# Scan and mixture of adapters on one core: transposes in pairs, stores in 8 KB rows, a copy in words

## The chip, the cores and the metric

The kernel runs on one core of a Trainium2 chip. The core has five engines that work side by side, each through its own list of instructions and in that list's order: TensorE (PE in the profile), VectorE (DVE), ScalarE (ACT), GpSimd (POOL) and SyncE (SP), which issues most of the transfers. Sixteen DMA engines carry them. The metric is the time of one execution on the device in microseconds; smaller is better. A time is given as the median of several runs.

## The reference

A linear recurrence over 8 sequences of 6400 tokens with 128 channels gives x, and a mixture of eight rank-16 adapters, two of them chosen for each token, is added to it:

```python
for t in range(S):
    h = a[:, t] * h + b[:, t]
    out[:, t] = h
...
logits = x @ w_gate
topk = np.argpartition(-logits, K, axis=1)[:, :K]
...
        z = x[mask] @ A[e]
        delta[mask] += w[mask, k, None] * (z @ B[e])
return (x + delta).astype(np.float32)
```

K is 2 and w is the softmax over the two largest logits. `a`, `b` and the output are float32 of 26.2 MB each, 51200 tokens by 128 channels.

## The kernel before

**Chunks.** The 51200 tokens are 100 chunks of 512. For a chunk c the work is a chain of small steps, and the program names each step by a family and a number:

- `la`, `lb`: the loads of a and b, a pair of chunks in each (512 KB, 128 partitions with a 4 KB row each, line 396). Six buffers of a and six of b; a load waits until PE has read the buffer's earlier pair. The first four chunks come singly.
- `A`, `B`: PE turns a chunk to channels by tokens with transposes against the identity, into two banks `pA` and two banks `pB` (line 417). From chunk 4 on, B of chunk c and A of chunk c+1 are woven into one step `P`c of 16 transposes: P4 is B4 with A5, P5 is B5 with A6. `P`c waits for the copy of A(c-1) and the scan of c-2, which free the banks.
- `ae`: ACT copies pA to SBUF (line 435). `sc`: DVE scans, out of that copy and of pB, into `xT` as 16-bit numbers (line 482), chunk after chunk.
- `Z`, `ze`: one matmul for each block of 128 tokens gives the eight adapters' inner vectors and the logits (line 500), six blocks in a unit; ACT copies them to the ring `zl` (line 506).
- `g1` to `g8`, `gx`, `w1`: the gates of a group of four units (24 blocks), in seven small steps on DVE or POOL and a sigmoid on ACT (lines 534 to 554).
- `mu`: the inner vectors times the gates, in 16 bits, POOL or DVE (line 569).
- `T`, `te`: PE transposes that in 16 bits (line 578), and ACT or DVE copies it from PSUM to `zwT` (lines 582 and 583, with the helper at line 300). `D`: x and the adapters' output are summed in PSUM with eight matmuls (lines 588 and 589). `T` and `D` share one of two banks `pO`.
- `oe`: ACT or DVE copies the bank to the ring `outt` (line 602, helper 300). `st`: SP stores it (line 631).

**Order.** Nothing is scheduled when it runs. `ORDER` (lines 28 to 100) lists for each engine the steps in the order in which it takes them, and where a step may run on either of two engines the list in which it stands decides (`te` and `oe` on ACT or DVE; `mu` and the gates on POOL or DVE). `Program.waits` derives the semaphore waits from the dependences. So an engine whose next step isn't ready holds up everything behind it in its list, and SP's list holds loads and stores together.

**Rings and stores.** `STORES` says how many chunks a store takes: 48 stores of two chunks and four of one. The tokens of a stored tile are dealt out in runs, one run to a partition, so that each partition stores one row: `Z` of a block therefore waits for the scans of the whole tile in which it lies. `NX`, `NZ` and `NO` are the sizes of the rings `xT` (24 chunks), `zl` (120 blocks) and `outt` (72 blocks). `SPLIT` cuts one store by partitions, 124 and 4. `FILL` puts four more PE transposes of the identity, read by nobody, ahead of the transposes of a for each of chunks 7 to 14 (`fi7` to `fi14`, line 446).

Of the kernel before, what the change touches and what calls it, by code (L numbers as in the profile page):

```python
# [12 lines left out]
STORES = [2] * 48 + [1] * 4  # L13
SPLIT = {68: [124, 4]}
TOP8 = 4
WARM = 16
FILL = {k: 4 for k in range(7, 15)}
# [3 lines left out]
NX = 24  # L21
NZ = 120
NO = 72
# [3 lines left out]
TAIL_CHUNKS = 12  # L27
ORDER = {
# [16 lines left out]
    ),  # L45
    "act": (
# [60 lines left out]
class Program:  # L107
# [18 lines left out]
    def schedule(self):  # L126
        named = {op.name: op for op in self.ops}
        assert len(named) == len(self.ops)
        self.order = {e: [named[name] for name in ORDER[e].split()] for e in self.ENGINES}
        assert sum(len(o) for o in self.order.values()) == len(self.ops)  # L130
        for e in self.ENGINES:
            n = 0
            for op in self.order[e]:
# [597 lines left out]
```

## Time and profile before

| | |
|---|---|
| time, median of 3 runs | 201.59 us (201.13 to 202.28) |
| the profiled execution, its time | 201.01 us |
| its span, from first to last instruction | 199.2 us |
| granted TensorE clock over the span | 0.994 |
| bytes moved by DMA | 79.26 MB |
| read from HBM, written to HBM | 52.56 MB, 26.21 MB |
| instructions | 7709 |

The profile is of one execution. Its first part gives each engine's busy time. The second cuts the span into 40 slices of 4.98 us. Another part lists the DMA queues with the number of their packets, the megabytes and the time these took as a share of sixteen engines' span. Groups of instructions are listed with what one of them takes. Views by stretch give the same busy times for any part of the span, where the column ahead of the last is the DMA engines' busy share; a share may come out a little over 1 because packets follow each other with a small overlap. A busy PE is modelled: matmuls are pipelined, and each is shown with its whole latency, so that the distance from one start to the next says more than the busy share.

### The profile page before, as it was taken

What the parts mean: (1) busy time and instruction counts of PE and PEld (TensorE: products, weight loads), DVE (VectorE), ACT (ScalarE), POOL (GpSimd) and SP (SyncE); (2) the same over time, 40 slices, a digit from 0 to 9 for tenths busy, and PEclk for the clock granted to TensorE, in tenths of its full rate; (3) what the DMA queues carried; (4) which work ended last, traced back from release to release, by engine and by line L of the source; (5) the groups of instructions that cost most, each with busy time, mean ns of one, the idle gap of its engine ahead of it and who ended that gap; (6) DMA issues with size and microseconds to landing.
All of it is one profiled execution on the core that took longest, in us unless ns stands there. A gap on an engine that the chain in (4) does not pass through costs nothing.

```text
span 199.2 us, 7709 instructions
## 1 busy us (share of the span) xinstructions
PE 185.2 (93%) x3224; PEld 165.5 (83%) x3224; DVE 175.0 (88%) x291; ACT 176.9 (89%) x327; POOL 136.0 (68%) x168
## 2 busy tenths in 40 slices
PE   6899999999998979999999999999999999999990
PEld 6778888889987968899989989889988978878970
DVE  1599999989999879799999999999999899899980
ACT  2378699999988979899999999999999989999981
POOL 3210186878786657969989998796598978676520
PEclk9999999999999999999999999999999999999997
DMA  5999999999999999999999999999999999999796
GB/s 214 385 414 406 410 407 407 409 406 410 411 410 413 414 411 412 415 414 408 414 415 406 411 410 416 411 411 415 414 412 414 417 410 412 406 393 392 298 405 254
DMA packets 22921, 79.26 MB, mean 398 GB/s; under 512 B 2664, under 2 KB 2920, under 8 KB 22888
## 3 DMA queue, kind: packets, MB, share of 16 engines
q1 hardware_dynamic: 22312, 78.39, 98.1%
q8 instruction: 25, 0.41, 0.8%
q10 hardware_dynamic: 576, 0.40, 0.6%
q14 instruction: 8, 0.07, 0.1%
HBM read 52.56 MB, written 26.21 MB: 395 GB/s over the span
## 4 chain that ended last, share of the span: by engine, by line
PE 80%; ACT 5%; DMA 4%; issue 3%; SPq 2%; POOL 2%; DVE 1%; DVEq 0%
PE pB L417 23%; PE pO L588 13%; PE pZ L500 13%; PE pO L578 12%; PE pO L589 10%; PE pA L417 5%; DMA a_tm<-in_a_dram 4%; ACT outt L300 3%; PE pA L446 2%; SPq L396 2%; POOL zw L569 2%; ACT zwT L300 1%; ACT a_st L435 1%; ACT zl L506 1%; DVE xT L482 1%
## 5 line engine op out<-in xcount | busy, mean ns | idle before, releaser
L482 DVE TENSOR_TENSOR_SCAN xT<-a_st,xT,pB 128x512 f16<-128x512 f32 x96 | 120.4, 1254 | 6.6 <-PE pA L417 3.1
L569 POOL TENSOR_TENSOR zw<-zl,g 128x512 f16<-128x512 f32 x90 | 94.5, 1065 | 29.2 <-DVE g L554 23.2
L417 PE MATMUL pB<-ident_f,b_tm 64*128 64x64 f32 (+1 forms) x784 | 67.5, 229 | 1.2 <-issue 0.5
L417 PE MATMUL pA<-ident_f,a_tm 64*128 64x64 f32 (+1 forms) x784 | 67.8, 229 | 0.6 <-issue 0.4
L435 ACT COPY a_st<-pA 128x512 f32<-128x512 f32 x100 | 59.0, 613 | 7.9 <-PE pA L417 7.2
L417 PEld LDWEIGHTS pB<-ident_f,b_tm 64*128 64x128 f32 (+1 forms) x784 | 55.8, 139 | 10.9 <-issue 3.4
L506 ACT COPY zl<-pZ 128x816 f32<-128x816 f32 (+1 forms) x69 | 58.1, 842 | 1.7 <-PE pZ L500 1.6
L588 PE MATMUL pO<-ident_h,xT 128*128 128x128 f16 x368 | 55.2, 233 | 2.0 <-issue 1.8
L417 PEld LDWEIGHTS pA<-ident_f,a_tm 64*128 64x128 f32 (+1 forms) x784 | 56.0, 139 | 1.2 <-DMA a_tm<-in_a_dram 0.7
L300 ACT COPY outt<-pO 128x512 f32<-128x512 f32 x87 | 52.2, 609 | 4.6 <-PE pO L589 4.1
L589 PE MATMUL pO<-cst_h,zwT 128*128 128x128 f16 x368 | 53.0, 219 | 1.7 <-issue 1.7
L588 PEld LDWEIGHTS pO<-ident_h,xT 128*128 128x128 f16 x368 | 46.3, 144 | 4.9 <-issue 2.1
L589 PEld LDWEIGHTS pO<-cst_h,zwT 128*128 128x128 f16 x368 | 39.6, 108 | 1.8 <-issue 1.8
L500 PE MATMUL pZ<-cst_h,xT 128*128 128x136 f16 x400 | 37.8, 229 | 0.5 <-issue 0.4
L578 PE MATMUL pO<-ident_h,zw 128*128 128x128 f16 x368 | 35.5, 220 | 1.1 <-POOL zw L569 0.4
L500 PEld LDWEIGHTS pZ<-cst_h,xT 128*128 128x128 f16 x400 | 30.6, 145 | 1.5 <-DVE cst_h L324 0.2
L578 PEld LDWEIGHTS pO<-ident_h,zw 128*128 128x128 f16 x368 | 22.3, 97 | 5.5 <-POOL zw L569 1.3
L300 DVE COPY zwT<-pO 128x512 f16<-128x512 f16 x56 | 23.0, 414 | 3.5 <-PE pO L578 3.1
L300 ACT COPY zwT<-pO 128x512 f16<-128x512 f16 x36 | 21.4, 600 | 0.9 <-PE pO L578 0.8
L545 POOL TENSOR_TENSOR L<-L,k 128x192 f32<-128x192 f32 x14 | 8.8, 631 | 4.6 <-DVE L L543 4.0
L482 DVE TENSOR_TENSOR_SCAN xT<-a_st,pB 128x512 f16<-128x512 f32 (+1 forms) x8 | 7.5, 938 | 4.5 <-PE pB L417 4.4
L548 POOL TENSOR_TENSOR k<-k,L 128x192 f32<-128x192 f32 (+1 forms) x17 | 9.1, 535 | 2.5 <-DVE L L539 1.8
(56 smaller groups left out, 120.0 us busy)
## 6 DMA issues: line engine op xcount, KB each, us to landing
a_tm<-in_a_dram SPq DMA_DIRECT2D x48, 512.0 KB, 13.3
b_tm<-in_b_dram SPq DMA_DIRECT2D x48, 512.0 KB, 13.4
out_dram<-outt SPq DMA_DIRECT2D x47, 512.0 KB, 11.9
a_tm<-in_a_dram SPq DMA_DIRECT2D x4, 256.0 KB, 4.9
out_dram<-outt SPq DMA_DIRECT2D x4, 256.0 KB, 4.0
b_tm<-in_b_dram SPq DMA_DIRECT2D x3, 256.0 KB, 5.6
out_dram<-outt SPq DMA_DIRECT2D x1, 496.0 KB
b_tm<-in_b_dram ACTq DMA_DIRECT2D x1, 256.0 KB, 4.0
```

Of the source, the lines that this page charges most:

```text
L300: return e.copy(dst, src) if e is eng["act"] else e.tensor_copy(dst, src)
L417: last = e.transpose(*args)
L435: lambda e: e.copy(a_st[c % NA][:, :], pA[:, c % 2, :]))
L482: last = e.tensor_tensor_scan(out=x[:, s0:s1], data0=a_st[c % NA][:, s0:s1], data1=pB[:, c % 2, s0:s1], initial=init, op0=ALU.mult, op1=AL ...
L500: last = e.matmul(pZ[:, k // (n // 2), o : o + W], xblock(b0 + k), Awg_h)
L506: lambda e: e.copy(zl[:, zb : zb + n, :].rearrange("p (h k) w -> p h (k w)", h=2), pZ[:, :, 0 : n // 2 * W]))
L545: d3 = wide(5, [d3], lambda e: e.tensor_tensor(out=ll, in0=ll, in1=kk, op=ALU.add))
L548: d6 = wide(7, [d2, d5], lambda e: e.tensor_tensor(out=kk, in0=kk, in1=ll, op=ALU.add))
L569: lambda e: e.tensor_tensor(out=wv, in0=zv, in1=gv, op=ALU.mult))
L578: last = e.transpose(ptile[:, k * 128 : k * 128 + 128], zz[:, k, :], ident_h[:, :])
L588: e.matmul(dst, xblock(b0 + k), ident_h[:, :], start=True, stop=False)
L589: last = e.matmul(dst, zt[:, k * 128 : k * 128 + 128], B_h, start=False, stop=True)
```

## The change

The diff has five parts.

1. `STORES` becomes [2,2], sixteen of four chunks, [2,2], six of four and four of one: 30 stores in place of 52. A store of four chunks has rows of 8 KB on each partition. The tiles of `xT` and `outt` follow. The rings become `NX` 32 chunks, `NO` 96 blocks, `NZ` 80 blocks.
2. `te` on ACT copies the 512 16-bit numbers of a partition as 256 words of 32 bits. On DVE it stays as it was.
3. `FILL` is two in place of four.
4. The lists of all five engines are new. On PE, P5 and P6, P7 and P8, and so on to P97 and P98 stand next to each other, so that A of both chunks of a transfer is turned in one stretch. By counting the lists: ACT has 69 `te` (38 before) and 82 `oe` (95); DVE has 31 `te` (62), 18 `oe` (5) and 15 `mu` (10); POOL has 85 `mu` (90); of the gates' steps g2, g3, g5, g6 and g7 DVE has 6, 11, 5, 7 and 8 (9, 6, 3, 7 and 5). PE goes from 32-bit to 16-bit operands or back 107 times (155).
5. `AHEAD`, `TREE` and `MASK` bring code that isn't reached with the values given (1000, empty, empty): no list of SP is 1000 steps long.

```diff
-STORES = [2] * 48 + [1] * 4
+STORES = [2,2]+[4]*16+[2,2]+[4]*6+[1]*4
-FILL = {k: 4 for k in range(7, 15)}
+FILL = {k:2 for k in range(7,15)}
-NX = 24
-NZ = 120
-NO = 72
+NX = 32
+NZ = 80
+NO = 96
 ORDER = {
     "pe": (
-        "P41 P42 D23 T24 Z26 P43 T25 D24 Z27 D25 T26 P44 P45 Z28 D26 T27 P46 Z29 T28 D27 D28 Z30 P47 T29 T30 P48 D29 "
+        "T23 Z25 T24 D23 D24 Z26 T25 T26 D25 P43 P44 T27 D26 D27 T28 Z27 P45 P46 T29 Z28 D28 D29 P47 P48 T30 T31 Z29 "
...
-        "Z60 D74 D75 P93 Z61 T77 T76 P94 P95 D76 D77 Z62 T78 P96 T79 Z63 D78 D79 T80 T81 Z64 D80 D81 P97 T82 Z65 T83 "
-        "D82 D83 T84 P98 T85 D84 Z66 D85 T86 B99 T87 Z67 T90 D86 D87 T91 Z68 T88 T89 D91 D88 D90 T92 D89 T93 T94 D92 "
+        "T75 P93 P94 T76 D75 Z60 D76 T77 P95 P96 T78 Z61 D77 D78 Z62 T79 T80 Z63 D79 D80 Z64 T81 P97 P98 T82 D81 D82 "
+        "T83 T84 D83 Z65 D84 T85 B99 D85 T86 Z66 T87 D86 D87 Z67 T88 T90 T91 T89 D88 Z68 D90 T93 D89 D91 T92 T94 D93 "
...
     "sp": (
-        "la20 la24 la22 st0 lb22 la26 lb24 lb26 la28 la30 lb30 st2 lb28 lb34 la32 la34 lb32 lb36 la36 st6 st4 lb38 "
+        "lb20 lb22 la22 la24 lb26 lb24 la26 la28 lb28 st2 st0 lb30 la30 la32 st4 lb32 la34 lb34 lb36 la36 la38 lb38 "
...
-        "la84 st46 lb84 st48 la86 la88 lb86 lb88 st50 la90 st52 lb90 st54 la92 lb92 la94 st56 lb94 la96 st58 lb96 "
-        "st60 la98 st62 st72 st64 lb98 st66 st68 st78 st76 st70 st74 st82 st80 st86 st84 st90 st88 st92 st94 st96 "
-        "st97 st98 st99 "
+        "la76 lb76 st32 la78 lb78 la80 lb80 la82 lb82 la84 lb84 st40 la86 lb86 la88 lb88 st44 la90 lb90 la92 lb92 "
+        "st48 la94 lb94 st52 la96 lb96 st56 la98 lb98 st60 st68 st70 st64 st72 st80 st76 st84 st88 st92 st97 st96 "
+        "st99 st98 "
...
-            o_te[c] = P.add("dve act", f"te{c}", J, [o_T[c]] + get(o_D, c - NW),
-                            lambda e: copy(e, zt, ptile[:, 0:C]))
+            o_te[c] = P.add("dve act", f"te{c}", J // 2, [o_T[c]] + get(o_D, c - NW),
+                            lambda e: e.copy(zt.bitcast(F32), bank[:, 0 : C // 2]) if e is eng["act"]
+                            else e.tensor_copy(zt, ptile[:, 0:C]))
```

More of the change, by code (lines that the diff above doesn't have):

```diff
@@ L12 @@
 GROUPS = [1, 2] + [4] * 15 + [2, 1, 1, 1, 1]
-STORES = [2] * 48 + [1] * 4
-SPLIT = {68: [124, 4]}
+STORES = [2,2]+[4]*16+[2,2]+[4]*6+[1]*4
+SPLIT = {68:[124,4]}
 TOP8 = 4
 WARM = 16
-FILL = {k: 4 for k in range(7, 15)}
+FILL = {k:2 for k in range(7,15)}
 HEAD = 4
@@ L27 @@
 TAIL_CHUNKS = 12
+AHEAD = 1000
+TREE = ()
+MASK = ()
 ORDER = {
     "pe": (
[15 rows of a table removed]
[15 rows of a table added]
     ),
     "act": (
[16 rows of a table removed]
[17 rows of a table added]
     ),
     "dve": (
[14 rows of a table removed]
[13 rows of a table added]
     ),
     "pool": (
[8 rows of a table removed]
[8 rows of a table added]
     ),
     "sp": (
[8 rows of a table removed]
[7 rows of a table added]
     ),
@@ L130, in schedule @@
         assert sum(len(o) for o in self.order.values()) == len(self.ops)
+        for before, op in zip(self.order["sp"], self.order["sp"][AHEAD:]):
+            op.deps = op.deps + [before]
         for e in self.ENGINES:
@@ L552, in gating @@
                     zlast[zpos[u] + k] = d5 if top else d2
-            o_g[gi] = wide(8, [a1, d5] + (get(o_mu, glast[gi - NG]) if gi >= NG else []),
-                           lambda e: e.scalar_tensor_tensor(
-                               out=gg, in0=ll, scalar=0.0, in1=sg, op0=ALU.is_ge, op1=ALU.mult))
+            free = get(o_mu, glast[gi - NG]) if gi >= NG else []
+            if gi in MASK:
+                d8 = wide(9, [d5, d6], lambda e: e.tensor_scalar(
+                    out=ll, in0=ll, scalar1=0.0, scalar2=1.0, op0=ALU.is_ge, op1=ALU.mult))
+                o_g[gi] = P.add("pool dve", f"gf_{gi}", nb, [a1, d8] + free,
+                                lambda e: e.tensor_tensor(out=gg, in0=ll, in1=sg, op=ALU.mult))
+            else:
+                o_g[gi] = wide(8, [a1, d5] + free, lambda e: e.scalar_tensor_tensor(
+                    out=gg, in0=ll, scalar=0.0, in1=sg, op0=ALU.is_ge, op1=ALU.mult))
         def back(gi, c):
```

108 rows, old and new, of the table ORDER are left out of this document.

## Prediction, before the result was known

> **What bounds the kernel now.** I read the page first: the DMA row of its slices and the queues, then the chain.
>
> ```profile
> span 199.2 us, 7709 instructions
> ...
> PE 185.2 (93%) x3224; PEld 165.5 (83%) x3224; DVE 175.0 (88%) x291; ACT 176.9 (89%) x327; POOL 136.0 (68%) x168
> ...
> DMA  5999999999999999999999999999999999999796
> GB/s 214 385 414 406 410 407 407 409 406 410 411 410 413 414 411 412 415 414 408 414 415 406 411 410 416 411 411 415 414 412 414 417 410 412 406 393 392 298 405 254
> ...
> q1 hardware_dynamic: 22312, 78.39, 98.1%
> ...
> PE 80%; ACT 5%; DMA 4%; issue 3%; SPq 2%; POOL 2%; DVE 1%; DVEq 0%
> ...
> a_tm<-in_a_dram SPq DMA_DIRECT2D x48, 512.0 KB, 13.3
> ```
>
> The queue that carries every load and store is busy for 98.1% of the span, and from the third slice to the thirty-fifth the rate never leaves 406 to 417 GB/s. That flatness is what to see: a transfer rate that doesn't move while the work on the engines changes is a ceiling. The chain names PE for 80%, but it follows one path only, and a load takes 13.3 us from issue to landing, ten times the 1.27 us that 512 KB need at 412 GB/s: about ten transfers stand in the queue. What PE releases late is late in a queue that isn't empty.
>
> Then the engines, stage by stage (PE, PEld, DVE, ACT, POOL with instructions, the clock, the DMA share, the rate).
>
> ```profile
> 90.00:110.00 20.00, 19.91 (x380) 18.24 (x379) 19.57 (x26) 19.98 (x38) 18.59 (x24) 1.00 1.02 411
> 110.00:130.00 20.00, 19.72 (x376) 17.91 (x375) 19.14 (x30) 19.66 (x38) 17.41 (x22) 1.00 1.03 412
> ...
> 170.00:180.00 10.00, 9.44 (x150) 7.88 (x148) 9.11 (x24) 9.50 (x18) 7.74 (x8) 1.00 0.99 398
> 180.00:190.00 10.00, 9.87 (x152) 9.14 (x153) 9.82 (x36) 10.00 (x23) 5.61 (x8) 1.00 0.86 345
> 190.00:199.20 9.20, 4.00 (x60) 3.24 (x57) 3.28 (x14) 4.14 (x10) 0.47 (x1) 0.88 0.83 324
> ```
>
> ACT and DVE are nearly full too, so compute is a close second, and in the last 20 us the order turns round: ACT is full (10.00 of 10) while the DMA share falls to 0.86. So DMA bounds the kernel up to about 172 us, and compute bounds the tail. The forecast is the DMA's work plus what the DMA idles at the end.
>
> **Stores in 8 KB rows: minus 1.8 us of DMA work.** No store of before has 8 KB rows, so I take the price of a row from two stretches, one with 4 KB rows only (60 to 80 us) and one with 2 KB rows (the last stores, 195 to 197 us).
>
> ```profile
> q1 hardware_dynamic: 2248, 8.19, 101.4%
> ```
>
> ```profile
> q1 hardware_dynamic: 416, 0.77, 101.3%
> ```
>
> 8.19 MB are 2000 rows of 4 KB; 1.014 x 16 engines x 20 us = 324.5 us of packet time, or 162.2 ns a row. 0.77 MB are 376 rows of 2 KB; 1.013 x 16 x 2 us = 32.4 us, 86.2 ns a row. Two rows of 2 KB cost 172.4, so joining two rows saves 10.2 ns. The change has 22 stores of four chunks, 22 x 128 = 2816 joins: 2816 x 10.2 ns / 16 engines = **1.8 us**. The bounds: nothing, if an 8 KB row moves as two pieces, and 2.0 us by the rounding of 0.77 MB (0.765 MB is 373.5 rows, 86.8 ns each, 11.4 ns a join). I take 1.8.
>
> The Trainium skill, DMA: Bandwidth & Descriptors, section "Why small descriptors are slow", puts the overhead at about 3 cycles a packet. At the 850 MHz that its section "Where 436 GB/s comes from" gives, an estimate by that page is 3.5 ns a join and 0.6 us in all; the rows show three times that, and the measurement decides.
>
> **The tail: minus 1.2 us.** The DMA view from 160 us to the end has slices of 0.98 us.
>
> ```profile
> GB/s 397 401 414 422 422 414 414 405 410 414 426 422 414 376 359 393 368 405 414 414 393 389 389 426 339 288 247 359 192 405 405 418 405 401 410 385 380 395 94 4
> ```
>
> Against 412 GB/s the nine low slices (376 359 393 368 at 173 to 177 us, 339 288 247 359 192 at 183 to 188) lack 787 GB/s of a slice: 787 / 412 x 0.98 = 1.9 us in which the DMA had nothing to send. SP's queue in that stretch:
>
> ```profile
> 158.68 6.11 SPq L631 DMA_DIRECT2D out_dram<-outt  x3
> 164.83 0.45 SPq L396 DMA_DIRECT2D b_tm<-in_b_dram  x1
> 165.32 30.18 SPq L631 DMA_DIRECT2D out_dram<-outt  x19
> ```
>
> The last load (lb98) goes out at 164.83, behind three stores that took 6.11 us. In the new list lb98 stands ahead of st60: 60 chunks are stored before it in place of 66, so the last input comes 6 x 0.64 = 3.8 us sooner (0.64 us is a chunk's 262 KB at 412 GB/s), and 40 chunks of stores remain to cover the rest of the compute instead of 34. Against it: PE's list has 19 `D` left behind P98 (D81 to D99) where it had 16. ACT's busy time after 180 us is 10.00 + 4.14 = 14.1 us for 16 chunks, 0.9 us each; three more are 2.7 us. Net 1.1 us sooner. I take 1.2 of the 1.9, bounds 0 and 1.9; st80 now stands ahead of st76, so a late oe83 would hold two stores.
>
> **What the edits do to the engines; worth nothing by itself while DMA is the bound.**
>
> ```profile
> L506 ACT COPY zl<-pZ 128x816 f32<-128x816 f32 x62 | 53.7, 867 | 1.1 <-PE pZ L500 1.0
> L300 ACT COPY outt<-pO 128x512 f32<-128x512 f32 x87 | 52.2, 609 | 4.6 <-PE pO L589 4.1
> L300 DVE COPY zwT<-pO 128x512 f16<-128x512 f16 x56 | 23.0, 414 | 3.5 <-PE pO L578 3.1
> L300 ACT COPY zwT<-pO 128x512 f16<-128x512 f16 x36 | 21.4, 600 | 0.9 <-PE pO L578 0.8
> L569 DVE TENSOR_TENSOR zw<-zl,g 128x512 f16<-128x512 f32 x10 | 6.8, 684 | 0.0
> L506 ACT COPY zl<-pZ 128x544 f32<-128x544 f32 x7 | 4.4, 624 | 0.6 <-PE pZ L500 0.6
> L446 PE MATMUL pA<-ident_f 128*128 128x128 f32 x32 | 5.0, 279 | 0.0
> L300 DVE COPY outt<-pO 128x512 f32<-128x512 f32 x5 | 3.4, 674 | 0.5 <-PE pO L589 0.5
> L547 DVE TENSOR_TENSOR L<-k,m 128x192 f32<-128x192 f32 x1 | 0.4, 352 | 0.0
> L357 ACT CAST cst_h<-pZ 128x128 f16<-128x128 f32 x1 | 0.3, 265 | 0.3 <-PE pZ L351 0.3
> ```
>
> ACT: a copy costs by elements, not bytes (512 of 16 bits 600 ns, of 32 bits 609), and (867 - 624) / 272 = 0.89 ns each. 256 words: 600 - 256 x 0.89 = 371 ns; bounds 265 (128 elements) and 600. `te`: 69 x 0.371 - 38 x 0.600 = +2.8 us; `oe`: -13 x 0.609 = -7.9. ACT falls by 5.1 us; at 600 ns a copy it would rise by 31 x 0.600 - 7.9 = 10.7.
>
> DVE: -31 `te` x 0.414 + 13 `oe` x 0.674 + 5 `mu` x 0.684 = -0.7 us, and seven more gate steps net of some 0.3 us, +2.1: 175.0 us (the page's busy time) becomes 176.4, level. POOL gives up five `mu` and seven gate steps and gets lighter. PE: the fillers halved are half of 5.0 us. Pairing removes switches between 32-bit and 16-bit operands, which PE's starts show (start, length, then the step):
>
> ```profile
> 100.62 0.22 PE L417 MATMUL pA<-ident_f,a_tm 64*128 64x64 f32 x1
> 100.62 0.22 PE L417 MATMUL pB<-ident_f,b_tm 64*128 64x64 f32 x1
> 100.68 0.22 PE L417 MATMUL pA<-ident_f,a_tm 64*128 64x64 f32 x1
> 100.68 0.22 PE L417 MATMUL pB<-ident_f,b_tm 64*128 64x64 f32 x1
> 100.84 0.40 PE L578 MATMUL pO<-ident_h,zw 128*128 128x128 f16 x4
> 101.07 0.23 PE L588 MATMUL pO<-ident_h,xT 128*128 128x128 f16 x1
> ```
>
> Starts are 60 ns apart within a kind, 160 across the switch: 48 switches fewer are 48 x 0.1 = 4.8 us of PE. DMA stands next behind PE, so that is slack, not time.
>
> SP: a store of four chunks waits for four `oe`, with all loads behind it. Early on the list has lb28 ahead of st2 and st0: loads of 30 chunks are 60 x 0.64 = 38 us of work for the queue, while D3 stands just behind P18, where before it came behind P21. I cost that at nothing; if the first stores came 2 us after the queue ran dry, that is 2 us.
>
> The rings: `zl` now holds three groups in place of five, and Z43 overwrites blocks of mu45, but T46 stands ahead of Z43 in PE's own list, so nothing new waits. The larger tiles of `xT` delay `Z` by up to two chunks; the lists put `Z` behind that.
>
> **The rivals.**
>
> - *A, the forecast.* Both terms: 201.01 - 1.8 - 1.2 = 198.0 on the scale of the profiled execution. The median of runs lies 0.58 above that execution: **198.6**. Chance 0.50.
> - *B, 8 KB rows save nothing*, only the tail does: 201.59 - 1.2 = 200.4. For it: no transfer of before shows such a row. Against: the two prices above. Chance 0.15, half of it within 0.5% of before. The Trainium skill, same page, section "SWDGE vs HWDGE vs iDMA", has packets of at most 4096 B as preferred, which would cut the rows and give B; no run so far shows a store's row cut.
> - *C, the tail keeps its idle*, the rows save 1.8: 199.8. Chance 0.15.
> - *D, the pairs stall the scans, slower.* P of the second chunk needs the scan of two chunks back, and it now follows the first directly; PE waits at it with `T` and `D` queued behind, and DVE then waits for the next pair. Two chunks take the DMA 1.573 MB / 412 GB/s = 3.82 us, and DVE 2 x 1.764 = 3.53 us of work (176.4 / 100). The joined rows take 0.04 off the 3.82. A wait of DVE under 0.25 us a pair is hidden; beyond 0.29 it costs 48 times the rest. At 0.35 it is 48 x 0.06 = 2.9 us: 204.5. For it: DVE is at 19.57 of 20 in one stage. Against, all 92 scans of a whole chunk together idled 6.2 us in before:
>
> ```profile
> L482 DVE TENSOR_TENSOR_SCAN xT<-a_st,xT,pB 128x512 f16<-128x512 f32 x92 | 117.4, 1276 | 6.2 <-PE pA L417 2.8 <-ACT a_st L435 1.6
> ```
>
>   Chance 0.14.
> - *E, the word copy takes 600 ns.* ACT would need 10.7 us more. Between 90 and 130 us it has 0.36 us to spare in 40, and 21 chunks there would bring 2.2; the other full stage, 180 to 190, about 8 chunks, 0.9: 201.6 + 1.9 + 0.9 - 1.8 = 202.6. Chance 0.06.
>
> **How the numbers follow.** A measurement here tells 0.5%, about 1 us, from no change. Faster by more: A 0.49 + C 0.15 + half of B = 0.71. Within: 0.12 (half of B, a little of A, D and E). Slower by more: 0.17 (D and E). The low end is 201.59 - 2.0 - 1.9 = 197.7, less 0.7 for the spread of runs (201.13 to 202.28): 197.0; the high end, 203.0, takes in E and D up to a wait of 0.32 us a pair (201.6 + 48 x 0.03 = 203.0).
>
> **What the profile after would show.** The rows right: q1 some 3200 packets fewer (the joins, and 22 stores fewer at 16 packets of their own), and a rate of about 416 GB/s in the middle slices at the same share; B if the rate stays at 412 or the packets don't fall. The tail right: no slice under 380 GB/s between 160 us and the last three. The word copy right: its group at 350 to 400 ns on ACT. D would show as PE's `pA` or `pB` steps waiting on DVE's `xT`, and scans idle by more than 12 us in all with the DMA share under 1.00 in the middle. What would make it wrong above all is a middle stage where the DMA share falls: then the DMA is no longer the bound.

## The result and the profile after

The changed kernel takes 209.27 us (median of 4 runs, 208.21 to 210.03), the kernel before beside it 201.49 us (201.13 to 202.28, 4 runs). The ratio is 1.0386, 95% interval 1.0355 to 1.0418: slower by 7.8 us where 3.0 us faster was forecast, and outside the range. A median in this document may hold one slower run (those of `b_stores`, `a_pool`, `o_free4`, `o_pairs2` and `o_words` do); the ratios leave such runs out. The profiled execution is the one of 210.03 us. In it the granted clock fell to half from 56.3 to 59.7 us; two of the other runs had the full clock throughout and spans of 206.4 and 206.9 us, so that this stretch explains some 1.5 us of that one execution and not the loss.

The page of the changed kernel, the lines that answer to those shown of before:

```profile
span 208.2 us, 7639 instructions
...
PE 186.7 (90%) x3208; PEld 164.5 (79%) x3208; DVE 179.1 (86%) x285; ACT 174.5 (84%) x345; POOL 125.0 (60%) x156
...
DMA  6999999999999799589999999999999999986986
GB/s 219 372 415 406 409 408 411 398 416 388 410 397 413 306 320 414 215 324 401 346 419 413 415 410 418 414 408 415 411 418 411 417 418 417 421 350 274 384 351 258
...
q1 hardware_dynamic: 19144, 78.39, 94.7%
...
PE 53%; DVE 20%; ACT 14%; issue 6%; DMA 3%; POOL 1%; ACTq 0%; DVEq 0%
...
a_tm<-in_a_dram SPq DMA_DIRECT2D x48, 512.0 KB, 11.8
```

Three things have changed. The rate is no longer flat: slices of 306, 320, 215, 324 and 346 GB/s stand between 68 and 104 us (a slice is 5.2 us now), and the last five are low. The chain, which was PE for 80%, goes through DVE for 20% and ACT for 14%: the end is set by hand-overs from one engine to the next. And no engine is as full as it was. The sign that the prediction named as what would make it wrong above all, a middle stage with a falling DMA share, is there. The stretches (PE, PEld, DVE, ACT, POOL, clock, DMA share, rate) put it in one table:

```profile
70.00:90.00 20.00, 18.84 (x344) 16.53 (x344) 17.27 (x24) 18.78 (x38) 15.39 (x18) 1.00 0.83 305
90.00:110.00 20.00, 19.18 (x368) 17.37 (x366) 18.98 (x25) 18.32 (x37) 13.26 (x16) 1.00 0.99 379
110.00:130.00 20.00, 19.15 (x354) 17.38 (x350) 19.25 (x28) 18.76 (x38) 16.35 (x22) 1.00 1.02 415
170.00:180.00 10.00, 9.29 (x162) 8.22 (x162) 9.04 (x15) 8.67 (x18) 7.75 (x9) 1.00 1.02 418
180.00:190.00 10.00, 9.19 (x142) 7.77 (x140) 8.88 (x22) 8.92 (x19) 6.59 (x8) 1.00 0.76 313
```

Between 90 and 130 us ACT was busy for 39.64 of 40 us before and for 37.08 now, DVE for 38.71 and 38.23. From 180 to 190 us the DMA idles a quarter of the time where it idled a seventh.

The groups that carry the terms of the sum, and the scans:

```profile
L486 DVE TENSOR_TENSOR_SCAN xT<-a_st,xT,pB 128x512 f16<-128x512 f32 x92 | 117.5, 1277 | 10.5 <-PE pA L421 6.9 <-PE pB L421 0.5 <-ACT a_st L439 0.3
L510 ACT COPY zl<-pZ 128x816 f32<-128x816 f32 x62 | 52.9, 853 | 3.8 <-PE pZ L504 3.6
L304 ACT COPY outt<-pO 128x512 f32<-128x512 f32 x75 | 44.2, 601 | 6.4 <-PE pO L600 5.7
L593 ACT COPY zwT<-pO 128x256 f32<-128x256 f32 x63 | 23.7, 385 | 3.1 <-PE pO L588 2.6
L594 DVE COPY zwT<-pO 128x512 f16<-128x512 f16 x29 | 12.0, 413 | 1.9 <-PE pO L588 1.6
L304 DVE COPY outt<-pO 128x512 f32<-128x512 f32 x17 | 11.5, 674 | 0.9 <-PE pO L600 0.9
L579 DVE TENSOR_TENSOR zw<-zl,g 128x512 f16<-128x512 f32 x15 | 11.3, 770 | 0.0
```

The copy in words takes 385 ns, 371 were forecast. `mu` on DVE takes 770 ns where it took 684. The 92 scans of whole chunks idle for 10.5 us where it was 6.2. The waits of the engines (total, times, longest) in the changed kernel, and below them the same waits of the kernel before:

```profile
ACT a_st L439 <- PE pA L421: 11.4, 15, 2.3
...
DVE xT L486 <- PE pA L421: 7.1, 15, 1.9
```

```profile
ACT a_st L435 <- PE pA L417: 7.2, 10, 1.7
...
DVE xT L482 <- PE pA L417: 3.1, 11, 0.8
```

And the waits of SP's queue, after and then before:

```profile
SPq L400 <- PE pA L421: 77.8, 39, 9.2
SPq L642 <- ACT outt L304: 36.5, 10, 11.9
```

```profile
SPq L396 <- PE pA L417: 36.1, 26, 4.3
SPq L631 <- ACT outt L300: 23.3, 13, 5.0
```

ACT and DVE wait longer for PE's transposes, and the queue of SP waits twice as long for PE to free a load buffer. That row is easily misread. It doesn't say that loads were late: the loads that land between 30 and 184 us in the changed kernel do so 1 to 15 us before PE first reads them (5.3 us in the median, 2.7 before), and no wait of PE in that time names a load. The loads were early and stood waiting for a buffer, because PE was late.

Where the 9.0 us of span came from can be read on DVE, whose work and idle time fill the span: 175.0 + 24.2 = 199.2 us before, 179.1 + 29.1 = 208.2 after. 4.1 us are more work, 4.9 are more idling.

### The profile page after: what moved, and what is told of

Its sections match the earlier page's. It is cut to its first block, busy times and chain, and to the rows that moved or that the text cites. A ratio compares the mean times of both kernels' runs of the same rounds, so it can differ in the third digit from the quotient of the medians.

```text
span 208.2 us, 7639 instructions
## 1 busy us (share of the span) xinstructions
PE 186.7 (90%) x3208; PEld 164.5 (79%) x3208; DVE 179.1 (86%) x285; ACT 174.5 (84%) x345; POOL 125.0 (60%) x156
## 4 chain that ended last, share of the span: by engine, by line
PE 53%; DVE 20%; ACT 14%; issue 6%; DMA 3%; POOL 1%; ACTq 0%; DVEq 0%
PE pB L421 14%; DVE xT L486 12%; PE pZ L504 9%; PE pO L599 8%; PE pO L588 7%; PE pA L421 6%; PE pO L600 6%; ACT outt L304 4%; ACT a_st L439 4%; ACT zl L510 4%; DVE zw L579 3%; DMA b_tm<-in_b_dram 3%; POOL zw L579 1%; ACT zwT L593 1%; DVE zwT L594 1%
## 5 line engine op out<-in xcount | busy, mean ns | idle before, releaser
L579 POOL TENSOR_TENSOR zw<-zl,g 128x512 f16<-128x512 f32 x85 | 89.2, 1069 | 37.0 <-DVE g L564 28.8
L421 PE MATMUL pB<-ident_f,b_tm 64*128 64x64 f32 (+1 forms) x784 | 65.2, 228 | 5.3 <-issue 2.2
L421 PE MATMUL pA<-ident_f,a_tm 64*128 64x64 f32 (+1 forms) x784 | 65.5, 229 | 0.9 <-issue 0.5
L510 ACT COPY zl<-pZ 128x816 f32<-128x816 f32 (+1 forms) x69 | 57.3, 830 | 4.6 <-PE pZ L504 4.3
L599 PE MATMUL pO<-ident_h,xT 128*128 128x128 f16 x368 | 53.9, 232 | 3.0 <-issue 2.3
L304 ACT COPY outt<-pO 128x512 f32<-128x512 f32 x75 | 44.2, 601 | 6.4 <-PE pO L600 5.7
L588 PE MATMUL pO<-ident_h,zw 128*128 128x128 f16 x368 | 34.2, 222 | 2.6 <-ACT outt L304 1.0
L593 ACT COPY zwT<-pO 128x256 f32<-128x256 f32 x63 | 23.7, 385 | 3.1 <-PE pO L588 2.6
L551 POOL TENSOR_TENSOR L<-k,m 128x192 f32<-128x192 f32 (+1 forms) x13 | 7.3, 562 | 12.4 <-DVE m L550 12.3
L594 DVE COPY zwT<-pO 128x512 f16<-128x512 f16 x29 | 12.0, 413 | 1.9 <-PE pO L588 1.6
L304 DVE COPY outt<-pO 128x512 f32<-128x512 f32 x17 | 11.5, 674 | 0.9 <-PE pO L600 0.9
```

The lines of the kernel that those rows point to most:

```text
L304: return e.copy(dst, src) if e is eng["act"] else e.tensor_copy(dst, src)
L421: last = e.transpose(*args)
L510: lambda e: e.copy(zl[:, zb : zb + n, :].rearrange("p (h k) w -> p h (k w)", h=2), pZ[:, :, 0 : n // 2 * W]))
L579: lambda e: e.tensor_tensor(out=wv, in0=zv, in1=gv, op=ALU.mult))
L588: last = e.transpose(ptile[:, k * 128 : k * 128 + 128], zz[:, k, :], ident_h[:, :])
L593: lambda e: e.copy(zt.bitcast(F32), bank[:, 0 : C // 2]) if e is eng["act"]
```

## The experiments

The theories are numbered in the texts on record. *1* puts the loss into the engines' lists (*1a*: the pairs starve DVE; *1b*: DVE is fuller; *1c*: the gates on POOL). *2* has the list of SP let the DMA run dry at 64 to 98 us. *3* blames tiles and stores of four chunks. Later, *1'* says that the lists as written lose time in hand-overs while the parts themselves do no harm, and *3'* that pairs and tiles cost time with any lists. Where no other is named, a ratio is to the kernel before in the same series.

### Is the DMA the bound at all?

Both kernels with every store cut to 64 of its 128 partitions, so that half of the output stays unwritten:

```diff
-            cuts = SPLIT.get(c, [128])
+            cuts = [64]
```

> The kernel of before, but each store sends only 64 of the 128 partitions: half of the output is left out, the engines do all their work. It asks whether the DMA bounds before, as the prediction had it. 13.1 MB fewer of 79.3 take 32 us off the DMA's work. If the DMA sets the time: 190 to 197 us, down to where the engines set it. If the engines and their lists set it: 200 to 201.5, with the DMA share well under 1.

> The changed kernel with half of the output left out in the same way. Theory 1 (the engines' lists set the time, the DMA idles as a consequence): 205 to 209.5 us. Theory 2 (SP's list lets the DMA idle from 64 to 98 us, and the work missed there comes back later): under 202, as the DMA has slack to make up for it.

Measured: the kernel before 198.83 us, ratio 0.9854 [0.9820, 0.9888]; the changed one 206.38 us, ratio 1.0244 [1.0188, 1.0300]. The page of the kernel before with half the stores:

```profile
span 197.3 us, 7708 instructions
...
DMA  6999999999999994999999999999999916568397
GB/s 218 372 415 406 411 404 407 401 387 408 413 410 410 411 409 142 327 409 414 414 407 386 392 405 400 394 409 388 331 407 390 388 52 141 184 147 175 71 199 159
...
q1 hardware_dynamic: 18992, 65.28, 89.8%
...
PE 87%; DVE 4%; issue 3%; ACT 3%; POOL 0%; POOLq 0%; DVEq 0%
```

The queue had 0.981 x 199.2 = 195.4 us of work on each engine and has 0.898 x 197.3 = 177.2: 18.2 us were taken away (32 were expected, but with half of the partitions a 4 KB row took 175.1 ns in the mean in place of 161.7), and from 158 us on the DMA moves under 200 GB/s. The time falls by 2.7 us only. So the flat rate was a real ceiling, but a second limit, the engines' lists, lay 2.7 us below it. And without that ceiling the changed kernel is still 206.38 - 198.83 = 7.5 us behind: nearly the whole loss of 7.8 us lies on the side of the engines, in their lists with the tiles and rings that these use, and not in the DMA.

### The parts, one by one

The copy in words into the kernel before (`b_words`), and out of the changed one (`a_nowords`):

```diff
-            o_te[c] = P.add("dve act", f"te{c}", J, [o_T[c]] + get(o_D, c - NW),
-                            lambda e: copy(e, zt, ptile[:, 0:C]))
+            o_te[c] = P.add("dve act", f"te{c}", J // 2, [o_T[c]] + get(o_D, c - NW),
+                            lambda e: e.copy(zt.bitcast(F32), bank[:, 0 : C // 2]) if e is eng["act"]
+                            else e.tensor_copy(zt, ptile[:, 0:C]))
```

> The kernel of before with one part of the change alone: te on ACT copies 256 words. Three theories of the 7.8 us loss. Theory 1, the lists: PE's pairs put two scans next to each other on DVE, copies of zwT behind them come late, D and the next pair behind those, so that the engines' own order costs the time. Theory 2, SP's list: stores stand too far behind loads, and the DMA idles from 64 to 98 us. Theory 3, tiles of four chunks: Z and the stores wait for four scans and four copies. None of the three puts a loss on the word copy: 199.5 to 201.8 us by all, the copy at 385 ns. Above 203 would speak for a fourth cause in the copy itself.

> The changed kernel with the word copy undone: 69 copies of zwT on ACT at 600 ns in place of 385, 15 us more of ACT work in lists that were made for the shorter ones. Theory 1 (engines): 212 to 220 us, since ACT at 174 us would get close to 188. If the DMA or SP set the time: 208 to 211.

Measured: 201.1 us, ratio 0.9974 [0.9948, 1.0000], and 212.85 us, ratio 1.0555 [1.0500, 1.0609]. In the kernel before, the words take 5.7 us off ACT (176.9 to 171.2) and next to nothing off the time; in the changed kernel, going back puts 11.6 us on ACT (174.5 to 186.1) and 3.6 us on the time. The part is a gain or neutral, never a loss.

Stores and tiles of two chunks in the changed kernel, each second store right behind the first (`a_store2`), and stores and tiles of four in the kernel before (`b_stores`, with the rings of the changed kernel, the merged stores at the place of the later one and seven steps moved back behind the scans for which they now wait):

```diff
-STORES = [2,2]+[4]*16+[2,2]+[4]*6+[1]*4
+STORES = [2] * 48 + [1] * 4
```

```diff
-STORES = [2] * 48 + [1] * 4
+STORES = [2, 2] + [4] * 16 + [2, 2] + [4] * 6 + [1] * 4
...
-P67 T47 Z43 T48 D47
+P67 T47 T48 Z43 D47
```

> The changed kernel with one part undone: stores of two chunks, 4 KB rows, tiles of two, each second store directly behind the first in SP's list; all five lists otherwise as after. Theory 3, tiles of four cost the time: 201 to 204 us. Theory 1 and theory 2: 207 to 211, since the lists hold the engines and SP as before; the rows cost up to 1.8 us more where the DMA is full.

> The kernel of before with the stores alone changed: four chunks in a store, tiles and rings (32 chunks, 80 and 96 blocks) as after; each pair of stores is merged at the later one's place in SP's list, and seven steps (Z3, Z30, Z43, Z51, Z54, Z59, g1_14) are moved back in their lists as far as the larger tiles force it. Theory 3, tiles of four cost the time: 204 to 208 us. Theory 1, the lists: 199.5 to 202.5, with 8 KB rows at about 315 ns each in place of 2 x 162. Theory 2 expects a loss only if the DMA share falls under 1.00 in the middle.

Measured: 207.56 us, ratio 1.0293 [1.0225, 1.0361], and 238.49 us, ratio 1.1827 [1.1727, 1.1928]. The larger tiles cost the changed kernel 1.7 us net at most: the two intervals just touch, and against its two runs at the full clock (208.21 and 208.74 us) it is 0.9 us. In lists that weren't written for them they cost 37 us.

The pairs alone, in PE's list of the kernel before (`b_pairs`: the second P of each pair from P15 on moved up behind the first), and in the changed kernel the reverse (`a_first`: the first P of each pair moved ahead, to the middle between two pairs):

```diff
-P41 P42 D23 T24 Z26 P43 T25 D24 Z27 D25 T26 P44 P45 Z28
+P41 P42 D23 T24 Z26 P43 P44 T25 D24 Z27 D25 T26 P45 P46 Z28
```

```diff
-P59 P60 T40 T39 Z37 D40 D39 Z38 P61 P62 T42 T41 Z39 D42 D41 P63 P64
+P60 T40 T39 Z37 P61 D40 D39 Z38 P62 T42 T41 Z39 P63 D42 D41 P64
```

> The kernel of before with PE's list alone changed: from P15 on the second P of each pair (P16, P18 and so on to P98) is moved up to stand directly behind the first. Theory 1, pairs cost by themselves: 204 to 208 us, scans idle by more than 10 us in all waiting for PE. Theories 2 and 3 (SP's list; tiles of four): 199 to 202 us, since 2-chunk stores and SP's list are those of before and PE switches operands less often.

> Theory 1 stands (the engines' lists set the time); open is what in them. Theory 1a, the pairs: PE's list has several T and D between two pairs, their copies wait on DVE behind both scans of the pair, and the next pair waits behind them in PE's list, so that DVE starves. Here the first P of each pair from P15 on is moved ahead to the middle of the steps that stand between two pairs (42 moves), the other lists as after. 1a: 202 to 206 us, the scans' idle time under 7 us. Theory 1b, the placement (DVE has 18 oe and 15 mu and is simply fuller): 207 to 210.

Measured: 233.95 us, ratio 1.1621 [1.1548, 1.1693], and 224.84 us, ratio 1.1170 [1.1114, 1.1225]. Pairing costs 32 us and unpairing costs 16 us. Either way one list was changed and four were not, and that is all that these two kernels show; *1a* in the form that I gave it, that the changed kernel gains by spreading the pairs, falls.

SP's list alone (`a_sp`: four stores moved ahead of loads, so that the DMA has work from 64 to 98 us):

```diff
-la50 lb50 lb52 la54 lb56 la52 la56 lb54 la58 lb60 la60 lb58 la62 lb62 lb64 st20 st16 la64 st24
+la50 lb50 st16 lb52 la54 st20 lb56 st24 la52 la56 lb54 la58 lb60 la60 lb58 la62 lb62 st28 lb64 la64
```

> The changed kernel with SP's list alone changed: st16, st20, st24 and st28 are moved ahead to where the trace of after shows their copies done (behind lb50, la54, lb56 and lb62), and st76 stands ahead of st80. Theory 2: the DMA share stays near 1.0 from 64 to 98 us and the time falls to 199 to 204. Theory 1: the DMA idles less there and more later, and the time stays at 207 to 210.

Measured: 210.7 us, ratio 1.0467 [1.0426, 1.0508]. The rate of this kernel:

```profile
GB/s 208 374 413 406 407 409 407 406 412 416 410 415 408 358 410 416 418 420 405 419 407 402 405 416 407 412 405 398 383 414 422 414 414 401 313 231 190 226 292 314
```

The holes between 68 and 104 us are gone, but for one slice of 358, and nothing is gained: what was moved earlier is missing after 177 us. The run has a loss of its own: la52 now stands behind stores, and PE waited 2.1 us for it at 94 us. So by itself it can't say that the holes were free. What does is that no load was late in the changed kernel, and that `a_half`, with half of the output to store, stays 7.5 us behind: the holes were a consequence, and *2* falls as the cause of the loss; a small part isn't excluded.

### One engine's work taken away

Three kernels leave out work of one engine of the changed kernel. `a_dve` copies half the columns in DVE's `oe` from chunk 24 on, `a_pool` multiplies half the adapters in POOL's `mu` from chunk 8 on, and `a_pe` leaves x out of the sum in `D`:

```diff
-                            lambda e: copy(e, ov, bank[:, :]))
+                            lambda e: copy(e, ov, bank[:, :]) if c < 24 or e is eng.get("act") else copy(e, ov[:, 0:256], bank[:, 0:256]))
...
-                            lambda e: e.tensor_tensor(out=wv, in0=zv, in1=gv, op=ALU.mult))
+                            lambda e: e.tensor_tensor(out=wv[:, :, 0:4, :], in0=zv[:, :, 0:4, :], in1=gv[:, :, 0:4, :], op=ALU.mult) if c >= 8 and e is eng.get("pool") else e.tensor_tensor(out=wv, in0=zv, in1=gv, op=ALU.mult))
...
-                    e.matmul(dst, xblock(b0 + k), ident_h[:, :], start=True, stop=False)
-                    last = e.matmul(dst, zt[:, k * 128 : k * 128 + 128], B_h, start=False, stop=True)
+                    last = e.matmul(dst, zt[:, k * 128 : k * 128 + 128], B_h, start=True, stop=True)
```

> The changed kernel with DVE's copies of outt (17 of its 18, all but the first) cut to half of the columns, so that part of the output is left out: some 17 x 0.27 = 4.6 us less DVE work. Theory 1b (DVE is the bound): minus 3.5 to 5 us, 204 to 206. Theory 1a: minus 0 to 2, 207 to 209.5.

> The changed kernel with POOL's products zw cut to half of the adapters (from chunk 8 on; part of the computation is left out): some 80 x 0.5 = 40 us less POOL work. If POOL's steps gate T and D (a third theory, 1c): under 206. Theories 1a and 1b: 207 to 210, as POOL is busy for 60% only.

> The changed kernel without the matmuls that add x to the output (400 of 3208; part of the computation is left out): about 400 x 0.06 = 24 us less PE work, the largest cut of one engine here. Theory 1a (PE's list holds the next pair behind T and D): D is shorter by half, so the pairs come 0.25 us sooner for each D: 200 to 205. Theory 1b: 207 to 210, PE being busy for 90% as shown but with 15 to 18 us of starts in 20.

| kernel | busy time of the engine, us | time, us | ratio to before |
|---|---|---|---|
| the changed kernel | | 209.27 | 1.0386 [1.0355, 1.0418] |
| `a_dve` | DVE 179.1 to 175.3 | 207.86 | 1.0323 [1.0290, 1.0355] |
| `a_pool` | POOL 125.0 to 91.8 | 207.04 | 1.0256 [1.0192, 1.0320] |
| `a_pe` | PE 186.7 to 166.9 | 205.24 | 1.0167 [1.0101, 1.0233] |
| `a_nowords` | ACT 174.5 to 186.1 | 212.85 | 1.0555 [1.0500, 1.0609] |

No engine's work alone accounts for the loss: 20 us less on PE bring 4.0 us, 33 us less on POOL some 2.6 by the ratios, and with DVE's work back at the level of before the kernel is still 6 us behind it. (What `a_pe` brings is limited by the DMA as well: its chain goes through the loads of b for 21%.) Each engine's work counts for a part, which is what a chain through all of them looks like. *1b* accounts for 1.4 us.

### All parts, with lists made anew

If the lists lose and the parts don't, then other lists should bring the parts' gain out. Four kernels have all five lists laid out again, step by step, with the durations that the groups of the two traces show: `o_pairs4` has all parts of the change (47 pairs on PE), `o_free4` all but that the pairs are free to part (13 remain, with 163 switches of operand width), `o_pairs2` pairs with stores and tiles of two, and `o_words` the kernel before with the words alone. An excerpt of PE's list of each:

```diff
-T23 P41 P42 D23 T24 Z26 P43 T25 D24 Z27 D25 T26 P44
+D20 P41 P42 T21 T22 Z25 D21 D22 P43 P44 T24 T23 Z26
...
+Z24 P41 T20 T19 Z25 D20 P42 P43 T22 Z26 D19 D22 P44
...
+T22 P41 P42 T21 D22 Z27 D21 P43 P44 T23 T24 Z28 D23
...
+Z26 P41 D19 P42 T20 T21 Z27 P43 D21 D20 P44 Z28 T22
```

> The changed kernel with all its parts kept (47 pairs next to each other on PE, stores of four chunks, word copies, fillers of two, rings), but with all five lists made anew by moving steps within and between lists against the durations and waits that the traces show. Theory 1' (the lists as written lose the time in hand-overs between the engines; the parts by themselves don't): 197 to 203 us. Theory 3' (pairs and tiles of four cost the time whatever the lists): 206 to 210.

> As o_pairs4, but the new lists need not keep the pairs together: 13 of 47 are left, PE switches operands 163 times. Theory 1' with harmless pairs: within 1 us of o_pairs4. If the pairs cost something even in good lists: 2 to 4 us less than o_pairs4, 195 to 199. Theory 3' (tiles of four): 203 or more.

> As o_pairs4 with pairs kept, but stores and tiles of two chunks, 4 KB rows. If tiles of four cost something in good lists: 1 to 3 us less than o_pairs4. If 8 KB rows gain something: 1 to 2 us more.

> The kernel of before with the word copy (rings, stores of two and fillers of four as before) and new lists made in the same way, pairs free. It asks whether the lists of before have the same room: if so, 194 to 199 us; if before's lists were already tight, 199.5 to 201.5.

Measured: 218.2 us, ratio 1.0823 [1.0752, 1.0894]; 218.64 us, 1.0853 [1.0798, 1.0909]; 217.71 us, 1.0797 [1.0728, 1.0866]; 215.11 us, 1.0667 [1.0594, 1.0741]. All four forecasts failed: none of my lists comes near those of the kernel before, not even with the parts of the kernel before, and so this doesn't show that the parts bring a gain in good lists. Beside each other the four differ little: with pairs or free, with tiles of four or of two, the times lie within 1 us or so, 3 us from the one without any of them, and all 13 us or more behind the old lists by the ratios. What the parts would do in lists that keep the DMA full, they don't say. Why my lists missed can be read in `o_words`. Its DVE is busy for 191.8 us instead of 175.0 and idles for 22.4 us, less than the 24.2 of before: the loss is longer work on DVE, not hand-overs. Most of it is that the same steps got slower in their new places, in these two groups for instance:

```profile
L564 DVE TENSOR_TENSOR zw<-zl,g 128x512 f16<-128x512 f32 x9 | 7.5, 832 | 0.1
L549 DVE SCALAR_TENSOR_TENSOR g<-L,sd 128x192 f32<-128x192 f32 x15 | 6.9, 459 | 0.0
```

In the kernel before with the copy in words, the same two groups take:

```profile
L569 DVE TENSOR_TENSOR zw<-zl,g 128x512 f16<-128x512 f32 x10 | 6.8, 684 | 0.0
L554 DVE SCALAR_TENSOR_TENSOR g<-L,sd 128x192 f32<-128x192 f32 x15 | 5.1, 338 | 0.8 <-ACT sd L549 0.7
```

9 x 148 ns and 15 x 121 ns are 3.1 us. The means hide what happened: seven of the nine `mu` took 660 to 694 ns and two 1311 and 1433; two of the fifteen others took 1181 and 1280, the rest 324 to 412. One of the long steps, and what POOL did beside it (start, length):

```profile
92.60 3.65 POOL L564 TENSOR_TENSOR zw<-zl,g 128x512 f16<-128x512 f32 x3
92.69 1.18 DVE L549 SCALAR_TENSOR_TENSOR g<-L,sd 128x192 f32<-128x192 f32 x1
```

In all of `o_words`, 22 steps of DVE other than scans took over 1.2 times the median of their shape in the kernels of old and changed lists, 13.6 us more than these medians together, and beside each of them POOL was at work for about half of its length or more, mostly with `mu`. The same count gives one step and 0.2 us in the kernel before, four and 1.4 us in the changed one, 17 and 7.1 us in `o_pairs4`, 22 and 12.5 us in `o_free4`. Not every step beside POOL is long (three of the seven short `mu` had POOL beside them throughout), and POOL's spans are rough in the profile. In `a_pool`, where POOL's `mu` are half as long, two of DVE's fifteen are long (1014 and 1056 ns); in the changed kernel three are (843, 1011 and 1505), with a mean of 770:

```profile
L579 DVE TENSOR_TENSOR zw<-zl,g 128x512 f16<-128x512 f32 x15 | 10.7, 727 | 0.1
```

The Trainium skill, GPSIMD Engine Reference, section "8. Key points", has POOL share its SBUF interfaces with VectorE and contend with DVE's instructions in a 2-port perf mode or with two SBUF inputs; the rows agree for the two groups above, which read two tensors from SBUF, while the copies out of PSUM kept their time (410 ns in `o_words`, 414 before). `L<-k`, which reads one tensor, was slowed too (486 ns in the mean, 250 before), and no run here shows why. A step's duration depends on what runs beside it, and a list laid out with mean durations doesn't know that. No run took these collisions away alone, and so the four kernels leave *1'* and *3'* undecided.

### Where in the lists

For each chunk the end of its scan, counted from the first instruction, can be set against that of `b_words`. In the changed kernel the lag is 0.6 us at chunk 10, 4.3 at 30, 4.6 at 60, 5.3 at 72, 8.0 at 75, 6.0 at 91, 9.1 at 93 and 9.2 at 99: it comes in steps, not evenly, and some of it is made good between them. (Some 1.5 us of the step at chunk 29 and just behind it are the half clock from 56.3 us.) `a_store2`, `a_dve` and `a_pool` step at the same chunks (28 to 29, 72 to 75, 91 to 93). Two kernels splice the lists of `a_store2` and `b_words`, which have the same stores, tiles and copies, ahead of P43 in PE's list, with what each other engine could have done by then: `h_ab` begins with the new lists and ends with the old, `h_ba` the other way round. Both have rings of `NX` 28, `NZ` 102 and `NO` 80. At the seam PE's list of `h_ab` is that of `a_store2` with

```diff
 Z26 T25 T26 D25
-P43 P44 T27 D26 D27 T28
+P43 Z27 P44 P45 Z28 D26
```

and PE's list of `h_ba` that of `b_words` with

```diff
 P42 D23 T24 Z26
-P43 T25 D24 Z27 D25 T26 P44
+D24 T25 T26 D25 P43 P44
```

> Stores and tiles of two chunks and the copy in words, as in both parents. All five lists are those of the changed kernel with stores of two (207.56 us) up to P42 and what can run by then, and from P43 on those of the kernel before with the copy in words (201.1 us). Against the second parent the scans of the first are late by 1.6 us at chunk 42 and by 5.3 at chunk 99. Local theory: the loss belongs to certain stretches of the lists, each stays where it was written: 201.1 + 1.6 = 202.7 us (201.5 to 204), and the scan of chunk 99 late by 1.6 us. Rival, the loss is a matter of how the parts fit as a whole (the backlog that the queues or the rings carry along): the second half loses as well, or the time is nearer to one of the parents by something else than the lag at the seam; 205 us or more.

> The other way round: the lists of the kernel before with the copy in words up to P42, and from P43 on those of the changed kernel with stores of two. Local theory: the steps in the scans' lag at chunks 72 to 75 (2.8 us) and 91 to 93 (2.4 us, in part made good between) and in the tail stay, those at chunks 13 to 14 and 28 to 29 are gone: 201.1 + 5.3 - 1.6 + 0.6 of the end = 205.4 us (204 to 206.5), and the same steps at the same chunks. Rival, the loss is a matter of the whole: the steps come at other chunks or vanish; 201 to 203 us or 207 and more.

Measured: `h_ab` 205.08 us, ratio 1.0180 [1.0152, 1.0209]; `h_ba` 205.86 us, ratio 1.0202 [1.0174, 1.0230]. `h_ba` came in the range of the local theory (205.4 forecast), but only in part by its steps: its scans lag by 0.4 us up to chunk 42, then by 2.9 at 72 and 4.8 at 75, by 3.5 at 91 and 5.8 at 93, and by 6.0 at the end, the steps of the new lists at the same chunks, 1.9 and 2.3 us where `a_store2` has 2.9 and 2.4. Between chunks 42 and 72 it lost 2.5 us where `a_store2` lost 1.0, and its lag at the end is 6.0 us where the theory has 3.7. `h_ab` came as the rival has it (205 us or more), not as the local theory (202.7). The first half did as expected (1.3 us late at chunk 42, with the steps at 13 to 14 and 28 to 29), but the old lists behind it, which lose nothing in their own kernel, lost another 3.3 us, 1.4 of them at chunk 61, where DVE stood empty waiting for PE. So the steps at 72 to 75 and at 91 to 93 go with their stretch of the lists, and a good stretch need not stay good behind another beginning. Whether the order in which the engines enter it does that, or the rings (102 blocks of `zl` where the old lists had 120), these two kernels don't show.

What such a step is shows DVE's timeline in the changed kernel (start, length) from the scan of chunk 91 to that of chunk 92:

```profile
168.72 1.27 DVE L486 TENSOR_TENSOR_SCAN xT<-a_st,xT,pB 128x512 f16<-128x512 f32 x1
169.91 0.67 DVE L579 TENSOR_TENSOR zw<-zl,g 128x512 f16<-128x512 f32 x1
170.49 0.25 DVE L547 TENSOR_SCALAR L<-k 128x192 f32<-128x192 f32 x1
170.66 0.35 DVE L564 SCALAR_TENSOR_TENSOR g<-L,sd 128x192 f32<-128x192 f32 x1
170.92 0.35 DVE L549 TENSOR_TENSOR L<-L,k 128x192 f32<-128x192 f32 x1
171.67 0.42 DVE L594 COPY zwT<-pO 128x512 f16<-128x512 f16 x1 [0.39 <-PE pO L588]
172.01 0.34 DVE L550 TENSOR_REDUCE m<-L 128x24 f32<-128x192 f32 x1
172.52 0.42 DVE L594 COPY zwT<-pO 128x512 f16<-128x512 f16 x1 [0.17 <-PE pO L588]
172.86 1.27 DVE L486 TENSOR_TENSOR_SCAN xT<-a_st,xT,pB 128x512 f16<-128x512 f32 x1
```

P91 and P92 were done by 169.15 us, but seven steps, 2.9 us with two waits for PE's T, stand ahead of the scan for which P93 and all behind it wait. The kernel before at the same chunks:

```profile
161.44 2.64 DVE L482 TENSOR_TENSOR_SCAN xT<-a_st,xT,pB 128x512 f16<-128x512 f32 x2
164.53 0.42 DVE L300 COPY zwT<-pO 128x512 f16<-128x512 f16 x1 [0.44 <-PE pO L578]
164.87 0.34 DVE L546 TENSOR_REDUCE m<-L 128x24 f32<-128x192 f32 x1
165.13 2.66 DVE L482 TENSOR_TENSOR_SCAN xT<-a_st,xT,pB 128x512 f16<-128x512 f32 x2
```

Here two steps stand between chunk 91 and chunk 92. Over the whole kernel the time from the end of one scan to the start of the next adds up to 50.2 us before, with two gaps over 2 us (chunks 96 and 98, 5.8 us together), and to 57.3 us after, with six (29, 43, 75, 92, 97 and 99, 16.7 us). Four of the six (75, 92, 97 and 99, 12.6 us) are clumps of six to nine short steps; `h_ba` has these four again (2.0, 2.1, 4.3 and 3.1 us). The other two have little work in them (0.3 and 1.1 us): at chunk 29 DVE waits for PE, which had issued nothing for 1.8 us with nothing to wait for that the profile shows.

What stays open: whether breaking up these clumps alone would bring the 7 us back. It wasn't tried, and `b_pairs`, `a_first` and `b_stores` say that a single list moved can cost more than it frees. Nor is it known how much of each step of the lag is the clump and how much the waits that follow it. The fillers and the rings weren't changed alone: the 1.1 us at chunk 14 are there in all kernels with the new beginning and two fillers (`h_ab` too) and in none with the old one and four. For the rings the changed kernel's waits speak against a part: none of 0.2 us or more is a copy to `zl` that waits for `mu` or one to `outt` that waits for a store.

## Why the prediction was wrong, point by point

- **The bound: wrong, and this is the step that failed.** "DMA bounds the kernel up to about 172 us" was true of the ceiling and wrong as a reason to count nothing else. Half the stores gone bought 2.7 us: the engines' lists stood 2.7 us below the DMA. From "ACT and DVE are nearly full too" I should have drawn that any change of the lists has at most that much cover. A queue at 98.1% shows one limit; it doesn't say how far the next one is.
- **"Worth nothing by itself while DMA is the bound": wrong.** All five lists were new, and I priced their contents (ACT -5.1, PE -4.8 us of switches, DVE level) but put their order at nothing. The contents came near the forecast: `te` on ACT +3.7 us and `oe` -8.5 (+2.8 and -7.9), the words 385 ns (371), though ACT's busy time fell by 2.4 us only, 176.9 to 174.5. With the DMA out of the way the engines' side cost 7.5 us. Of this the tiles account for at most 1.7 and DVE's added work for 1.4; the rest I put to the order of the lists, by what is left and by the steps that the splices carried along.
- **DVE 176.4 us: wrong by size**, 179.1. `mu` on DVE took 770 ns instead of 684 in the mean (1.3 us over 15 of them, all in three long steps beside POOL's work). `oe` and `te` came as forecast (+8.8 and -12.9 us), the gates at +2.4 for +2.1; the remaining 1 us is in no group's length. With DVE's work cut to 175.3 us only 1.4 us came back, so that this is the smaller part.
- **8 KB rows: the price right, the gain absent.** q1 has 3168 packets fewer (some 3200 forecast), and where the queue is full the rate is 412 to 418 GB/s (412 before, 416 forecast). In the packets' records a row of 8192 bytes takes 309 ns in the median and one of 4096 bytes 159, so that a join saves 9 ns (10.2 forecast). That speaks against rival B; the Trainium skill, DMA: Bandwidth & Descriptors, section "SWDGE vs HWDGE vs iDMA", prefers packets of at most 4096 B, without saying that longer rows are cut, and here 2816 rows of 8192 B moved whole. Yet the queue's whole work rose, from 195.4 us to 0.947 x 208.2 = 197.2: rows of 4 KB took 165.4 ns in the mean where they took 161.7. And tiles of four make `Z` and the stores wait for four chunks: 0.9 to 1.7 us net loss (`a_store2`) for a term of -1.8. The prediction's estimate by the Trainium skill, same page, section "Why small descriptors are slow", is 3.5 ns a join; the median rows don't agree.
- **The tail: wrong.** The DMA share from 180 to 190 us fell from 0.86 to 0.76. I had counted the loads that come sooner, not the lists of DVE: nine steps ahead of the scan of chunk 97 and nine ahead of that of chunk 99. lb98 did go out 4.0 us sooner (160.8 us for 164.8), but it landed at 180.0 us (178.2 before), and PE first read it at 184.5: a sooner load has no worth where PE is late. The sum had a miscount too: before, 68 chunks were stored ahead of lb98, not 66, and 32 remained, so that by its own terms the load came 8 x 0.64 = 5.1 us sooner, 2.4 net, and the term would have been the whole 1.9. By the DMA shares of the two low stretches, 0.95 and 0.75 beside 1.02 just ahead of them, even that is nearer to 1.6.
- **Rival D: the right sign, another mechanism.** It had the pairs stall the scans, 0.35 us each, evenly. Its sign in the middle came (a DMA share of 0.83), but the scans of whole chunks idled 10.5 us, under the 12 us that it named, PE's transposes of b waited for DVE's `xT` for 1.3 us in all, and the lag came in a few steps. The equal times of new lists with pairs and with free transposes (218.2 and 218.64 us) don't clear the pairs, since `o_free4` lost 5.4 us more to long steps of DVE; what the pairs cost in the changed kernel stays open. I gave 0.17 to all slower cases because I looked for one price per pair. Five hand-written lists made new at once were a risk of their own, and no rival held it.
- **Early stores costed at nothing: right.** The queue didn't run dry ahead of st2 and st0: the DMA share from 30 to 50 us is 1.03.

## What to carry to other kernels

When a queue or an engine reads 98%, ask how far below it the next limit lies before you call other edits free; a kernel that leaves out half of that work (here half the stores) answers it in one run. In a kernel of lists in fixed order, the order is a cost of its own: count, for the step on which the others wait (here the scan), what stands ahead of it on its engine each time, and look for clumps, not for averages. A change of PE's list that the others don't follow cost 16 and 32 us here, larger stores in lists not made for them 37, so that parts can't be priced by carrying them over one at a time. And where a group's mean has moved, look at its single instructions: here a few were two to three times as long, and the rest as before.

## What the runs showed of the hardware that was not expected

- PE stood for up to 1.9 us ahead of one instruction with nothing that the profile shows to wait for ("issue"), 1.77 us of it inside D11. The row of the changed kernel:

```profile
PEld pO L599 <- issue: 3.4, 3, 1.9
```

- In `b_pairs` such time grew to 30.8 us over 40 places; whether it hides there the wait for a scan wasn't shown:

```profile
PEld pB L416 <- issue: 30.8, 40, 1.7
```

- `mu` on DVE took from 684 to 850 ns in the mean with the same shape: 684 before, 727 beside a POOL with half the work, 770 in the changed kernel, 850 in `o_pairs4`. In the changed kernel that is twelve of 668 to 687 ns and three of 843, 1011 and 1505, each with POOL at work beside it.
- The granted clock fell to half for 3.4 us in the changed kernel (at 56.3 us), in `a_sp` (96.8), in `a_nowords` (40.9) and twice in `b_pairs` (35.9 and 145.1), each time 2.3 to 3.7 us after the start of a stop of PE of 0.9 to 2.1 us (1.8 us in the changed kernel). Other stops of 1.2 to 1.5 us, one of 1.4 in the kernel before at 70.8 us among them, weren't followed by one.
- Taking 13.1 MB of stores away left the rate of the rest near 400 GB/s up to 158 us in most slices (142 and 327 stand at 74 to 84 us, 331 at 138 to 143): the transfers that remained ran ahead instead of slower.
